# Engine order fixed through v and u of batch 1, and w_out's pieces placed one per two u tiles

## Chip, core, metric

One core of a Trainium2 chip runs the kernel. The metric is the device time of one execution in microseconds; lower is better. The engines are TensorE (PE; its weight loads are PEld), VectorE (DVE), ScalarE (ACT), GpSimd (POOL), and SyncE (SP), which issues the DMAs. Each works through its own list of instructions in order; semaphores make one wait for another.

## What is computed

A retention layer (8 batches, 8 heads, 576 positions, 64 features per head) feeds a gated MLP. Cut to what matters:

```python
scores = q @ k.T / 8                    # per batch and head
ret = (scores * Dmat[h]) @ v            # Dmat: gamma_h ** (i - j) for i >= j, else 0
x = heads side by side                  # (8, 576, 512)
h = np.maximum(x @ w_in, 0.0)           # w_in: 512 x 1024
u, v = h[..., :512], h[..., 512:]
v_n = (v - mean(v)) / np.sqrt(var(v) + 1e-06)        # over the 512 features
v_s = np.einsum('ts,bsd->btd', w_spatial, v_n) + b_spatial[None, :, None]
out = (u * v_s) @ w_out                 # w_out: 512 x 512
```

## The kernel before

Every product of the MLP is done in a reduced float format with each operand split into a high and a low part, and three matmuls (high x high, high x low, low x high; `mm3`) for each pair of tiles. A batch passes these stages:

- *retention* (`scores`, `prep`, `burst`, `evac`): five chunks of up to 128 positions. `burst` is the chunk's group of small matmuls on TensorE; its first ones need the chunk's keys, which GpSimd has scaled in place (`prep`; the tile is `qkv`, the factors `kd`), and `prep` also scales the queries (`qsc`).
- *v* (`v_steps`): blocks of 128 positions (four and a tail of 64, block 4). A block is 12 matmuls of 512 columns (8 for the tail) into one PSUM buffer `v_b_sb`, then seven steps on the same buffer: Relu (ACT), `BN_STATS` and `BN_AGGR` (DVE), root of the variance (ACT) and `mean - v` (ACT), the reciprocal and three small products for the scale (DVE; tile `sm`), the high part of the normalized v (ACT, tile `vn0`), and the low part (DVE, tile `vn1`). With this last step the buffer is free. The tail block adds two halves first and writes `vt1`, `vt2`.
- *u* (`u_tile`): eight tiles of 128 features x 288 positions, 12 matmuls each into a PSUM buffer, then a Relu on ScalarE which empties it.
- *vs* (`vs_mm`) and *f* (`f_stage`): the spatial product with the gate, and the product with `w_out`, eight tiles each.

v, u, vs and f share four PSUM buffers (pool `ps_m`, 512 columns each). A tile's first matmul waits until the tile that had the buffer before is done with it.

The weights come as 64-bit floats and are turned into the high and low format on the chip, in pieces of 128 columns: `front` (absolute value of the high words on ScalarE, a clamp on GpSimd), `mid` (three bit operations on VectorE, tile `f`), `back` (a cast to the high part on ScalarE, the low part on GpSimd). `w_out` has four such pieces, numbered 0 to 3, kind 2. They are `f_20` to `f_23` in the lists below, and `wout0`, `wout1` are the high and low results.

Until the end of batch 0's last gated u tile the order of TensorE, VectorE, ScalarE and GpSimd is the order in which the code is written (`Engine` records it as long as `ordered[0]` is true). From line 643 on a scheduler decides, by its own estimate of times, with all instructions behind the written part (`issue_after`); TensorE's retention matmuls keep their program order. Before the change the scheduled part starts ahead of v of batch 1, so in v and u of batch 1 it places the rest of w_out: `wout_work` (lines 631 to 639) gives one of its parts after each of the eight u tiles in program order, but nothing binds it to that place. After u of batch 1 come `f` of batch 0, with the retention of batch 2 woven in (`interleave`), then vs and f of batch 1, and so on to batch 7, which has no retention beside it.

Of the kernel before, what the change touches and what calls it, by code (L numbers as in the profile page):

```python
# [23 lines left out]
NC = S // C  # L24
# [3 lines left out]
NMB = DM // P  # L28
# [5 lines left out]
def retention_gmlp(ctx, tc, qkv, q_x, qk_t, q_xt, v_t, w_in, w_sp, b_sp, w_out, amask, qscale, kdec, sdec, out):  # L34
# [153 lines left out]
    def front(kind, i, clamp=po):  # L188
        words = staged[kind, i].rearrange("p (n two) -> p n two", two=2)
        hw, lw = words[:, :, 1], words[:, :, 0]  # L190
        f = early[:, i] if kind == 1 else sp.tile([P, 512], F32, name=f"f_{kind}{i}", tag="f", bufs=3)
        a = f if clamp is po else ps_m.tile([P, 512], F32, name=f"w_{kind}{i}", tag="m")
        ac.activation(out=a, in_=hw.bitcast(F32), func=AF.Abs)
        if clamp is po:
            po.tensor_scalar(out=a, in0=a, scalar1=2.0 ** -15, scalar2=None, op0=ALU.max)
        part[kind, i] = hw, lw, a, f

    def mid_steps(kind, i):
        hw, lw, a, f = part[kind, i]
        direct = kind == 1 and a is not f  # L200
        ps = a if kind != 1 or direct else ps_m.tile([P, 512], F32, name=f"w_{kind}{i}", tag="m")
        part[kind, i] = f, ps
        fi = ps.bitcast(I32)
        if direct:
            ve.tensor_scalar(out=a, in0=a, scalar1=2.0 ** -15, scalar2=None, op0=ALU.max)
        ve.tensor_scalar(out=fi, in0=a.bitcast(I32), scalar1=3, scalar2=0x3FFFFFFF, op0=ALU.logical_shift_left, op1=ALU.bitwise_and)
        ve.scalar_tensor_tensor(out=fi, in0=hw, scalar=-2 ** 30, in1=fi, op0=ALU.bitwise_and, op1=ALU.bitwise_or)
        yield
        ve.scalar_tensor_tensor(out=fi, in0=lw, scalar=29, in1=fi, op0=ALU.logical_shift_right, op1=ALU.bitwise_or)
        yield  # L210

    def mid(kind, i):
        for _ in mid_steps(kind, i):
            pass

    def back(kind, i, eng=po):
        hi, lo = (w[:, i, DH:] if kind == 1 else w[:, :, i * P:(i + 1) * P] for w in (win if kind < 2 else wout))
        f, ps = (t if kind == 1 else t.rearrange("p (a n) -> p a n", a=NCB) for t in part[kind, i])
        ac.copy(out=hi, in_=ps)
        if eng is po and kind == 1:  # L220
            ac.copy(out=f, in_=ps)
        eng.tensor_tensor(out=lo, in0=f if eng is po else ps, in1=hi.bitcast(F32), op=ALU.subtract)
# [118 lines left out]
    def mm3(ps, w, r, start, stop):  # L341
        pe.matmul(ps, w[0], r[0], start=start, stop=False)
        pe.matmul(ps, w[0], r[1], start=False, stop=False)
        pe.matmul(ps, w[1], r[0], start=False, stop=stop)

    def v_steps(b, sb):
        n = C if sb < NC else TL
        x = xs[b]
        pf = ps_m.tile([P, 512], F32, name=f"v_{b}_{sb}", tag="m")
        ps = pf[:n]  # L350
        t = slice(sb * C, sb * C + n)
        if sb < NC:
            for cb in range(NCB):
                if cb == 2 and (b, sb) == (0, 3):
                    yield
                mm3(ps, [x[:, i, cb, t] for i in range(2)], [win[i][:, cb, DH:] for i in range(2)], cb == 0, cb == NCB - 1)
        else:
            for cb in range(NCB):
                for i in range(2):
                    pe.matmul(pf, xt[:, cb], win[i][:, cb, DH:], start=(cb == 0 and i == 0), stop=(cb == NCB - 1 and i == 1))  # L360
        yield
        if sb == NC:
            tl = wk.tile([P, DH], F32, name=f"vl_{b}", tag="vl", bufs=1)[:TL]
            ac.copy(out=tl, in_=pf[TL:])
            ve.tensor_tensor(out=ps, in0=ps, in1=tl, op=ALU.add)
        ac.activation(out=ps, in_=ps, func=AF.Relu)
        yield
        s6 = wk.tile([P, 6], F32, name=f"s6_{b}_{sb}", tag="s6", bufs=3)[:n]
        ve.bn_stats(out=s6, in_=ps)
        mv = wk.tile([P, 2], F32, name=f"mv_{b}_{sb}", tag="mv", bufs=3)[:n]  # L370
        ve.bn_aggr(out=mv, in_=s6)
        s = wk.tile([P, 5], F32, name=f"sm_{b}_{sb}", tag="sm", bufs=3)[:n]
        ac.activation(out=s[:, 0:1], in_=mv[:, 1:2], func=AF.Sqrt, bias=eps[:n])
        ac.activation(out=ps, in_=ps, func=AF.Identity, scale=-1.0, bias=mv[:, 0:1])
        yield
        r = s[:, 1:2]
        ve.reciprocal(out=r, in_=s[:, 0:1])
        ve.tensor_scalar(out=s[:, 2:3], in0=mv[:, 1:2], scalar1=EPS, scalar2=r, op0=ALU.add, op1=ALU.mult)
        ve.tensor_scalar(out=s[:, 3:4], in0=s[:, 2:3], scalar1=r, scalar2=0.5, op0=ALU.mult, op1=ALU.mult)
        ve.tensor_scalar(out=s[:, 4:5], in0=s[:, 3:4], scalar1=-1.5, scalar2=r, op0=ALU.add, op1=ALU.mult)  # L380
        nrstd = s[:, 4:5]
        if sb < NC:
            hi, lo = vn[0][:, sb], vn[1][:, sb]
        else:
            hi, lo = vt1[:TL], vt1[TL:]
        ac.activation(out=hi, in_=ps, func=AF.Copy, scale=nrstd)
        if sb == NC:
            ac.activation(out=vt2[:TL], in_=ps, func=AF.Copy, scale=nrstd)
        yield
        ve.scalar_tensor_tensor(out=lo, in0=ps, scalar=nrstd, in1=hi.bitcast(F32), op0=ALU.mult, op1=ALU.subtract)  # L390
        yield

    def v_block(b, sb):
        for _ in v_steps(b, sb):
            pass
# [10 lines left out]
    def u_tile(b, db, t):  # L406
        ps = ps_m.tile([P, 512], F32, name=f"u_{b}_{db}_{t}", tag="m")[:, :HALF]
        u_mm(b, db, t, ps)
        u_relu(b, db, t, ps)

    def u_stage(b):
        for db in range(NDB):
            for t in range(2):
                u_tile(b, db, t)
                yield 1.6

    def v_stage(b):
        for sb in range(NC + 1):
            v_block(b, sb)
            yield 2.75 if sb < NC else 1.9  # L420
# [58 lines left out]
    def go(gen, n=1):  # L479
        for _ in range(n):  # L480
            next(gen)
# [32 lines left out]
    v = [v_steps(0, sb) for sb in range(NC + 1)]  # L514
# [113 lines left out]
    gated_u(1, 3)  # L628
    split_g(1)

    def wout_work():
        for i in range(1, NMB):
            if i > 1:
                front(2, i)
                yield
            mid(2, i)
            yield
            back(2, i)
            yield

    work = wout_work()
    g0 = xs[0]
    ordered[0] = False
    for eng in (pe, ve, ac, po):
        ctx.enter_context(tc.issue_after(eng.last))

    for _ in v_stage(1):
        pass
    for _ in u_stage(1):
        next(work, None)  # L650
    for b in range(1, B):
        interleave(main(b), retention(b + 1) if b + 1 < B else [], 50.0 if b > 1 else 40.0, 12.5)

# [76 lines left out]
```

## Time and profile before

| | us |
|---|---|
| executions timed | 556.49, 556.87, 857.03 (median 556.87) |
| the profiled execution | 556.34 |
| its span, first to last instruction | 554.6 |
| granted TensorE clock, mean over the span | 0.988 |

One execution was profiled. A row of the timeline gives the start and the duration of an instruction, or of a few equal ones that follow each other, in us from the span's start, with the engine, the operation and the tiles (output <- inputs, their numbers left out). All instructions stand at line 71, the helper through which they are issued, so they are told apart by their tiles. Square brackets hold the idle time of the engine ahead of the row and what ended it. A row of the windows gives busy time and number of instructions of PE, PEld, DVE, ACT and POOL in a stretch, then the granted TensorE clock, the share of the DMA engines and GB/s.

### The profile page before, as it was taken

What the parts mean: (1) busy time and instruction counts of PE and PEld (TensorE: products, weight loads), DVE (VectorE), ACT (ScalarE), POOL (GpSimd) and SP (SyncE); (2) the same over time, 40 slices, a digit from 0 to 9 for tenths busy, and PEclk for the clock granted to TensorE, in tenths of its full rate; (3) what the DMA queues carried; (4) which work ended last, traced back from release to release, by engine and by line L of the source; (5) the groups of instructions that cost most, each with busy time, mean ns of one, the idle gap of its engine ahead of it and who ended that gap; (6) DMA issues with size and microseconds to landing.
All of it is one profiled execution on the core that took longest, in us unless ns stands there. A gap on an engine that the chain in (4) does not pass through costs nothing.

```text
span 554.6 us, 15310 instructions
## 1 busy us (share of the span) xinstructions
PE 533.7 (96%) x6735; PEld 496.1 (89%) x6735; DVE 272.1 (49%) x588; ACT 207.8 (37%) x447; POOL 135.1 (24%) x133
## 2 busy tenths in 40 slices
PE   5898999499999999999999999999999999999997
PEld 4677998499998899989999899988999899998997
DVE  7786577812632735237351654427353373506240
ACT  4366335532223632236222552226322362226422
POOL 3857759501302120202102120121201122000000
PEclk8999999799999999999999999999999999999999
DMA  8992663004444322533234222342225341020002
GB/s 315 377 330 77 233 186 115 0 12 154 140 130 153 103 80 64 193 116 116 50 96 176 84 96 50 119 158 83 92 52 182 112 153 50 2 76 11 2 1 86
DMA packets 37045, 64.08 MB, mean 116 GB/s; under 512 B 14833, under 2 KB 27249, under 8 KB 33010
## 3 DMA queue, kind: packets, MB, share of 16 engines
q1 hardware_dynamic: 36978, 63.10, 34.5%
q8 instruction: 53, 0.87, 0.6%
q14 instruction: 14, 0.11, 0.1%
HBM read 53.65 MB, written 9.44 MB: 114 GB/s over the span
## 4 chain that ended last, share of the span: by engine, by line
PE 87%; DVE 4%; DMA 4%; ACT 2%; issue 1%; POOL 1%; SPq 0%; ACTq 0%
PE vs L71 22%; PE f L71 19%; PE u L71 18%; PE v L71 14%; PE r L71 14%; DMA qkv<-in_qkv 4%; DVE f L71 2%; DMA raw<-in_w_out 1%; DVE s L71 1%; ACT v L71 1%; DVE sm L71 0%; DVE w L71 0%; DVE vn L71 0%; ACT wtl L71 0%; POOL qsc L71 0%
## 5 line engine op out<-in xcount | busy, mean ns | idle before, releaser
L71 PE MATMUL vs<-wsp,vn 128*128 128x288 f32 x768 | 114.5, 297 | 1.2 <-ACT pre L71 0.5
L71 PE MATMUL u<-x,win 128*128 128x288 f32 x768 | 107.2, 299 | 8.2 <-DVE vn L71 6.6
L71 PEld LDWEIGHTS u<-x,win 128*128 128x128 f32 x768 | 104.3, 190 | 10.2 <-DVE vn L71 7.0
L71 PEld LDWEIGHTS vs<-wsp,vn 128*128 128x128 f32 x768 | 105.3, 188 | 2.9 <-DVE vn L71 0.7
L71 PE MATMUL v<-win,x 128*128 128x512 f32 x384 | 93.3, 398 | 0.0
L71 PE MATMUL f<-g,wout 128*128 128x288 f32 x672 | 92.1, 295 | 0.0
L71 DVE TENSOR_TENSOR at<-r,am 128x1024 f32<-128x1024 f32 (+1 forms) x40 | 44.5, 1113 | 95.2 <-PE r L71 95.2
L71 PEld LDWEIGHTS f<-g,wout 128*128 128x128 f32 x672 | 89.7, 188 | 0.5
L71 PEld LDWEIGHTS v<-win,x 128*128 128x128 f32 x384 | 71.0, 188 | 16.6
L71 POOL TENSOR_TENSOR qsc<-qsc,qs 128x512 f32<-128x512 f32 (+1 forms) x31 | 36.6, 1183 | 189.1 <-DMA qsc<-in_q_x 139.4
L71 PEld LDWEIGHTS r<-qkv 64*64 64x64 f32 x2176 | 45.8, 135 | 13.8 <-issue 6.3
L71 PE MATMUL r<-qkv 64*64 64x64 f32 (+1 forms) x2176 | 52.3, 235 | 5.4 <-POOL qkv L71 3.5
L71 DVE BATCH_NORM_STATS2 s<-v 128x6 f32<-128x512 f32 (+1 forms) x40 | 27.8, 694 | 57.6 <-ACT v L71 56.4
L71 ACT COPY o<-f 128x288 f32<-128x288 f32 x64 | 25.6, 400 | 73.4 <-PE f L71 73.4
L71 ACT CAST g<-vs 128x288 fp32r<-128x288 f32 x56 | 22.3, 399 | 74.2 <-DVE vs L71 73.0
L71 POOL TENSOR_TENSOR qkv<-qkv,kd 128x512 f32<-128x512 f32 x32 | 33.5, 1048 | 34.9 <-DMA qkv<-in_qkv 30.3
L71 ACT CAST x<-r 128x512 fp32r<-128x512 f32 x32 | 18.8, 586 | 59.6 <-DVE st L71 59.6
L71 DVE TENSOR_TENSOR g<-vs,g 128x288 fp32r<-128x288 f32 x56 | 25.6, 457 | 26.3 <-ACT g L71 26.3
L71 PE MATMUL r<-at,qkv 64*64 64x64 f32 (+1 forms) x1152 | 36.9, 225 | 0.5 <-DVE at L71 0.5
L71 DVE TENSOR_TENSOR vs<-vs,u 128x288 f32<-128x288 f32 x56 | 26.0, 464 | 22.7 <-PE vs L71 22.7
L71 POOL TENSOR_TENSOR st<-st,sd 128x256 f32<-128x256 f32 x24 | 14.9, 620 | 86.9 <-DVE st L71 86.8
L71 ACT ACTIVATE u<-u 128x288 f32<-128x288 f32 x56 | 22.4, 408 | 34.3 <-PE u L71 34.1
(73 smaller groups left out, 520.6 us busy)
## 6 DMA issues: line engine op xcount, KB each, us to landing
qkv<-in_qkv SPq DMA_DIRECT2D x31, 1024.0 KB, 5.3
out<-o SPq DMA_DIRECT2D x64, 144.0 KB, 1.8
qsc<-in_q_x SPq DMA_DIRECT2D x24, 256.0 KB, 3.3
raw_v<-in_w_in SPq DMA_DIRECT2D x4, 512.0 KB, 6.6
qkv<-in_qk_t SPq DMA_DIRECT2D x8, 256.0 KB, 3.7
qkv<-in_v_t SPq DMA_DIRECT2D x16, 128.0 KB, 3.2
raw<-in_w_in SPq DMA_DIRECT2D x4, 512.0 KB, 8.9
raw<-in_w_out SPq DMA_DIRECT2D x4, 512.0 KB, 3.6
```

The costliest lines, as they stand in the source:

```text
L71: ins = op(*args, **kw)
```

## The change

The written order now goes on through v and u of batch 1. `go(gen, n)` takes n steps of a generator; `v_steps` yields after the matmuls, after the Relu, after the statistics with root and shift, after the scale and high part, and after the low part. So block sb runs up to its statistics, then block sb - 1 does its low part, then block sb its scale and high part. The `front` of pieces 2 and 3 of w_out follows the last block's high part. The last block's low part stands behind the first u tile, and then w_out's `mid` and `back` alternate behind the following u tiles. The scheduler decides from f of batch 0 on.

```diff
@@ -628,26 +628,27 @@
     gated_u(1, 3)
     split_g(1)
 
-    def wout_work():
-        for i in range(1, NMB):
-            if i > 1:
-                front(2, i)
-                yield
-            mid(2, i)
-            yield
-            back(2, i)
-            yield
-
-    work = wout_work()
     g0 = xs[0]
+    v = [v_steps(1, sb) for sb in range(NC + 1)]
+    for sb in range(NC + 1):
+        go(v[sb], 3)
+        if sb:
+            go(v[sb - 1])
+        go(v[sb])
+    front(2, 2)
+    front(2, 3)
+    for n, _ in enumerate(u_stage(1)):
+        if n == 0:
+            go(v[NC])
+        elif n == 6:
+            back(2, 3)
+        elif n < 7:
+            i = (n + 1) // 2
+            (mid if n % 2 else back)(2, i)
     ordered[0] = False
     for eng in (pe, ve, ac, po):
         ctx.enter_context(tc.issue_after(eng.last))
 
-    for _ in v_stage(1):
-        pass
-    for _ in u_stage(1):
-        next(work, None)
     for b in range(1, B):
         interleave(main(b), retention(b + 1) if b + 1 < B else [], 50.0 if b > 1 else 40.0, 12.5)
 
```

The tiles in the lists below: `v_1_0` to `v_1_4` are batch 1's v blocks, `sm_1_n` and `mv_1_n` their small tiles, `u_1_d_t` its u tiles, all with a running number behind; `u_633` is u's result, `qkv_2_0` the first chunk of batch 2.

ScalarE through the first blocks of v of batch 1, before:

```order
L71 CAST wout0_1054<-f_21_1087 128x4x128
L71 ACTIVATE v_1_0_1239<-v_1_0_1239 128x512
L71 ACTIVATE sm_1_0_1257<-mv_1_0_1255,eps_91 128x1
L71 ACTIVATE v_1_0_1239<-v_1_0_1239,mv_1_0_1255 128x512
L71 ACTIVATE v_1_1_1266<-v_1_1_1266 128x512
L71 ACTIVATE vn0_343<-v_1_0_1239,sm_1_0_1257 128x512
L71 ACTIVATE sm_1_1_1284<-mv_1_1_1282,eps_91 128x1
L71 ACTIVATE v_1_1_1266<-v_1_1_1266,mv_1_1_1282 128x512
L71 ACTIVATE v_1_2_1293<-v_1_2_1293 128x512
L71 CAST wout0_1054<-f_22_1421 128x4x128
L71 ACTIVATE v_1_3_1320<-v_1_3_1320 128x512
```

and now:

```order
L71 ACTIVATE v_1_0_1239<-v_1_0_1239 128x512
L71 ACTIVATE sm_1_0_1257<-mv_1_0_1255,eps_91 128x1
L71 ACTIVATE v_1_0_1239<-v_1_0_1239,mv_1_0_1255 128x512
L71 ACTIVATE vn0_343<-v_1_0_1239,sm_1_0_1257 128x512
L71 ACTIVATE v_1_1_1265<-v_1_1_1265 128x512
L71 ACTIVATE sm_1_1_1283<-mv_1_1_1281,eps_91 128x1
L71 ACTIVATE v_1_1_1265<-v_1_1_1265,mv_1_1_1281 128x512
L71 ACTIVATE vn0_343<-v_1_1_1265,sm_1_1_1283 128x512
L71 ACTIVATE v_1_2_1292<-v_1_2_1292 128x512
```

The casts of w_out are gone from between v's steps, and each block's Relu stands behind the previous block's high part (`vn0`), where Relus of blocks 1 to 3 stood ahead of it.

VectorE in the middle of v of batch 1, before:

```order
L71 TENSOR_SCALAR f_22_1421<-f_22_1421 128x512
L71 TENSOR_SCALAR sm_1_1_1284<-mv_1_1_1282,sm_1_1_1284 128x1
L71 SCALAR_TENSOR_TENSOR f_22_1421<-raw_22_942,f_22_1421 128x512
L71 TENSOR_SCALAR sm_1_1_1284<-sm_1_1_1284 128x1
L71 BN_STATS s6_1_2_1307<-v_1_2_1293 128x6
L71 SCALAR_TENSOR_TENSOR f_22_1421<-raw_22_942,f_22_1421 128x512
L71 TENSOR_SCALAR f_23_1471<-f_23_1471 128x512
L71 TENSOR_SCALAR sm_1_1_1284<-sm_1_1_1284 128x1
L71 BN_AGGR mv_1_2_1309<-s6_1_2_1307 128x2
L71 SCALAR_TENSOR_TENSOR f_23_1471<-raw_23_1052,f_23_1471 128x512 x2
L71 BN_STATS s6_1_3_1334<-v_1_3_1320 128x6
L71 SCALAR_TENSOR_TENSOR vn1_344<-v_1_1_1266,sm_1_1_1284,vn0_343 128x512
```

and now, from block 1's statistics to block 2's scale (the low parts are the rows `vn1_344`):

```order
L71 BN_STATS s6_1_1_1279<-v_1_1_1265 128x6
L71 BN_AGGR mv_1_1_1281<-s6_1_1_1279 128x2
L71 SCALAR_TENSOR_TENSOR vn1_344<-v_1_0_1239,sm_1_0_1257,vn0_343 128x512
L71 RECIPROCAL sm_1_1_1283<-sm_1_1_1283 128x1
L71 TENSOR_SCALAR sm_1_1_1283<-mv_1_1_1281,sm_1_1_1283 128x1
L71 TENSOR_SCALAR sm_1_1_1283<-sm_1_1_1283 128x1 x2
L71 BN_STATS s6_1_2_1306<-v_1_2_1292 128x6
L71 BN_AGGR mv_1_2_1308<-s6_1_2_1306 128x2
L71 SCALAR_TENSOR_TENSOR vn1_344<-v_1_1_1265,sm_1_1_1283,vn0_343 128x512
L71 RECIPROCAL sm_1_2_1310<-sm_1_2_1310 128x1
L71 TENSOR_SCALAR sm_1_2_1310<-mv_1_2_1308,sm_1_2_1310 128x1
L71 TENSOR_SCALAR sm_1_2_1310<-sm_1_2_1310 128x1 x2
```

w_out's bit operations (`f_22`, `f_23`) stood between v's steps, and block 1's low part behind block 3's statistics; now it is behind block 2's statistics, and the bit operations are behind the last block.

GpSimd behind the splitting of batch 0's gate, before:

```order
L71 TENSOR_TENSOR qkv_2_0_1145<-qkv_2_0_1145,kd_75 128x512
L71 TENSOR_SCALAR f_22_1421<-f_22_1421 128x512
L71 TENSOR_SCALAR f_23_1471<-f_23_1471 128x512
L71 TENSOR_TENSOR qkv_2_1_1217<-qkv_2_1_1217,kd_75 128x512
L71 TENSOR_TENSOR wout1_1055<-f_21_1087,wout0_1054 128x4x128
L71 TENSOR_TENSOR qsc_2_1_1219<-qsc_2_1_1219,qs_74 128x512
L71 TENSOR_TENSOR qsc_2_2_1618<-qsc_2_2_1618,qs_74 128x512
L71 TENSOR_TENSOR wout1_1055<-f_22_1421,wout0_1054 128x4x128
L71 TENSOR_TENSOR wout1_1055<-f_23_1471,wout0_1054 128x4x128
```

and now:

```order
L71 TENSOR_SCALAR f_22_1373<-f_22_1373 128x512
L71 TENSOR_SCALAR f_23_1376<-f_23_1376 128x512
L71 TENSOR_TENSOR wout1_1055<-f_21_1087,wout0_1054 128x4x128
L71 TENSOR_TENSOR wout1_1055<-f_22_1373,wout0_1054 128x4x128
L71 TENSOR_TENSOR wout1_1055<-f_23_1376,wout0_1054 128x4x128
L71 TENSOR_TENSOR qkv_2_0_1145<-qkv_2_0_1145,kd_75 128x512
L71 TENSOR_TENSOR qkv_2_1_1217<-qkv_2_1_1217,kd_75 128x512
L71 TENSOR_TENSOR qsc_2_1_1219<-qsc_2_1_1219,qs_74 128x512
L71 TENSOR_TENSOR qsc_2_2_1618<-qsc_2_2_1618,qs_74 128x512
```

All of w_out's clamps and low parts now stand ahead of the scaling of batch 2's keys (`qkv_2_0`), which stood first. TensorE's list and SyncE's list of DMAs have the same order as before. In batches 2, 3, 5 and 6 a `vn` step and the neighbouring step on the retention's state (`st`) changed places on ScalarE and on VectorE.

## Prediction

> **What bounds the kernel now.** I began with the busy times and the costliest groups, to see which engine ends the span and where it waits.
>
> ```profile
> PE 533.7 (96%) x6735; PEld 496.1 (89%) x6735; DVE 272.1 (49%) x588; ACT 207.8 (37%) x447; POOL 135.1 (24%) x133
> ...
> L71 PE MATMUL u<-x,win 128*128 128x288 f32 x768 | 107.2, 299 | 8.2 <-DVE vn L71 6.6
> ```
>
> TensorE is busy for 96% of the 554.6 us, so only its idle time and its slow time can be won. Of the 8.2 us that it idles ahead of u's matmuls, 6.6 end with a write of `vn` by VectorE. TensorE's timeline from batch 1's v to the first burst of batch 2's retention has that wait:
>
> ```profile
> 85.08 11.36 PE L71 MATMUL v<-win,x 128*128 128x512 f32 x48
> 96.28 2.01 PE L71 MATMUL v<-win,xt 128*128 128x512 f32 x8
> 104.89 3.25 PE L71 MATMUL u<-x,win 128*128 128x288 f32 x12 [6.60 <-DVE vn L71]
> 108.79 11.39 PE L71 MATMUL u<-x,win 128*128 128x288 f32 x84 [0.65 <-ACT u L71]
> ...
> 124.30 1.36 PE L71 MATMUL r<-qkv 64*64 64x64 f32 x64
> ```
>
> The columns are start, duration, instructions, and in brackets the idle time ahead. v's matmuls end at 98.29 (96.28 + 2.01). Nothing runs until 104.89. The first u tile (12 matmuls) then takes 3.25 us, and after 0.65 us more of waiting the other seven run through: 11.39 / 7 = 1.63 us each. The windows over the gap show the clock in the column ahead of the DMA share (0.00 there):
>
> ```profile
> 98.30:101.40 3.10, 0.00 (x0) 0.00 (x0) 3.10 (x5) 2.06 (x5) 3.10 (x3) 1.00 0.00 0
> ...
> 104.80:108.20 3.40, 3.25 (x12) 2.90 (x12) 3.20 (x14) 2.06 (x5) 0.77 (x1) 0.50 0.00 0
> ```
>
> The clock is still 1.00 through the first 3.10 us of idling, and 0.50 through the stretch of 3.4 us in which the first u tile runs. So the place loses 6.60 + 0.65 + (3.25 - 1.63) = 8.87 us. No more than this can be won.
>
> Why TensorE waits: there are four PSUM buffers for v and u, and a v block gives its buffer back with its last step, the VectorE write of `vn`. u's first tile needs block 1's buffer. VectorE's timeline shows that step at 104.10, and what stands ahead of it, the w_out pieces (`f`):
>
> ```profile
> 85.65 1.69 DVE L71 TENSOR_SCALAR f<-f 128x512 int32<-128x512 int32 x1
> 87.38 2.82 DVE L71 SCALAR_TENSOR_TENSOR f<-raw,f 128x512 int32<-128x512 int32 x2
> ...
> 100.37 3.20 DVE L71 SCALAR_TENSOR_TENSOR f<-raw,f 128x512 int32<-128x512 int32 x2
> ...
> 104.10 0.73 DVE L71 SCALAR_TENSOR_TENSOR vn<-v,sm,vn 128x512 fp32r<-128x512 f32 x1
> ```
>
> ScalarE, before and behind the gap (the last two rows serve below):
>
> ```profile
> 90.23 0.62 ACT L71 CAST wout<-f 128x512 fp32r<-128x512 f32 x1 [2.64 <-DVE f L71]
> 90.75 0.58 ACT L71 ACTIVATE v<-v 128x512 f32<-128x512 f32 x1
> ...
> 108.54 0.68 ACT L71 ACTIVATE vn<-v,sm 128x512 fp32r<-128x512 f32 x1
> 109.11 0.28 ACT L71 ACTIVATE sm<-mv,eps 64x1 f32<-64x1 f32 x1
> ```
>
> Block 0's Relu starts at 90.75, behind a cast of w_out that waited for VectorE, though its matmuls (a quarter of 11.36 us) were done at about 88. From 100.37 to 103.57 VectorE was at the last piece of w_out, while v's blocks waited.
>
> **The change, part by part.** The instructions are the same; TensorE's and SyncE's order is the same, so no DMA is issued past another. The new order moves three things.
>
> *v without w_out in it.* In the new order each engine runs a block's steps in a fixed chain: Relu, statistics, root and shift, reciprocal and scale, `vn` high on ScalarE, the next block's Relu behind it, and the previous block's `vn` low on VectorE behind the next block's statistics. Batch 7's v runs with nothing beside it, so I take the steps' distances from there. TensorE, ScalarE, VectorE:
>
> ```profile
> 497.91 11.37 PE L71 MATMUL v<-win,x 128*128 128x512 f32 x48
> ```
> ```profile
> 500.97 0.58 ACT L71 ACTIVATE v<-v 128x512 f32<-128x512 f32 x1 [2.42 <-PE v L71]
> ...
> 503.77 0.58 ACT L71 ACTIVATE v<-v 128x512 f32<-128x512 f32 x1 [0.39 <-PE v L71]
> ...
> 511.16 0.58 ACT L71 COPY vl<-v 64x512 f32<-64x512 f32 x1 [0.67 <-PE v L71]
> ...
> 512.54 0.55 ACT L71 ACTIVATE v<-v 64x512 f32<-64x512 f32 x1
> ...
> 516.99 1.26 ACT L71 ACTIVATE vt<-v,sm 64x512 fp32r<-64x512 f32 x2 [0.62 <-DVE sm L71]
> ```
> ```profile
> 502.32 0.18 DVE L71 BATCH_NORM_AGGREGATE mv<-s 128x2 f32<-128x6 f32 x1
> 502.86 0.16 DVE L71 RECIPROCAL sm<-sm 128x1 f32<-128x1 f32 x1 [0.36 <-ACT sm L71]
> ...
> 503.31 0.46 DVE L71 TENSOR_SCALAR sm<-sm 128x1 f32<-128x1 f32 x2
> ...
> 507.95 0.18 DVE L71 BATCH_NORM_AGGREGATE mv<-s 128x2 f32<-128x6 f32 x1
> 508.05 0.72 DVE L71 SCALAR_TENSOR_TENSOR vn<-v,sm,vn 128x512 fp32r<-128x512 f32 x1
> 508.68 0.15 DVE L71 RECIPROCAL sm<-sm 128x1 f32<-128x1 f32 x1
> ...
> 513.85 0.17 DVE L71 BATCH_NORM_AGGREGATE mv<-s 64x2 f32<-64x6 f32 x1
> ...
> 516.45 0.45 DVE L71 TENSOR_SCALAR sm<-sm 64x1 f32<-64x1 f32 x2
> 518.28 0.74 DVE L71 SCALAR_TENSOR_TENSOR vt<-v,sm,vt 64x512 fp32r<-64x512 f32 x1 [1.38 <-ACT vt L71]
> ```
>
> From TensorE's start to block 0's Relu: 500.97 - 497.91 = 3.06. In the new kernel v's matmuls start at 85.08 as before, since all ahead of them is unchanged, so the Relu R0 = 88.14. From Relu to the second statistics step: 502.32 - 500.97 = 1.35. Block 0 has no earlier block's write to place: reciprocal at R + 1.89 (502.86), end of the scale steps at R + 2.80 (503.31 + 0.46), `vn` high 0.09 later (516.45 + 0.45 to 516.99), the next Relu 0.57 after that starts (108.54 to 109.11): R1 = R0 + 3.46 = 91.60. A later block has the previous `vn` low in between: it starts 0.10 behind the statistics (507.95 to 508.05), takes 0.72, and the reciprocal follows 0.63 after its start (508.68). That makes R + 2.08, scale steps until R + 2.99, high part R + 3.08, next Relu R + 3.65. So R2 = 95.25, R3 = 98.90. The previous block's buffer is free at R + 1.35 + 0.10 + 0.72 = R + 2.17: block 0's at 93.77, before block 4 needs it (96.28); block 1's at 97.42, before v ends; block 2's at 101.07.
>
> Block 4: the copy 0.57 behind block 3's high part (101.98) at 102.55; Relu 1.38 later (511.16 to 512.54), 103.93; second statistics 1.31 later (513.85), 105.24; block 3's low part 105.34 to 106.06; scale steps until 105.97 + 0.91 = 106.88; its high part 106.97; its low part 1.29 later (516.99 to 518.28), 108.26 to 109.00.
>
> *u.* TensorE starts 0.06 after a buffer is free (104.10 + 0.73 to 104.89). Tile 1 runs from 98.29 without a wait. Tile 2 starts at 101.13, tile 3 at 106.12, tile 4 at 109.06; with 1.63 us each the idle times are 1.21, 3.36 and 1.31. From tile 5 on the buffers come from u's own Relus, which are ready: the first one stands behind block 4's two high parts (106.97 + 1.26) and two Abs of w_out, which I take at 0.6 each as a high part: about 109.4, against 110.69. Before, tile 4 was the third of the free seven and started at 108.79 + 2 x 1.63 = 112.05. So the gain at tile 4 is 3.0 us, and the same five tiles follow.
>
> *The clock.* The longest gap, 3.36 us, exceeds the 3.10 after which the clock fell before, so I expect half clock once. Bounds: 0 if it lies inside a gap or doesn't come, 1.6 if a whole tile runs in it as before (3.25 - 1.63). If it lies from 106.1 to 109.5, as long as the stretch above, tile 3 takes 1.6 longer, of which the 1.31 gap behind it hides all but 0.3, and tile 4 loses 0.2: I take 0.5. [...]
>
> *w_out's pieces 1 to 3 beside u.* They still lie beside TensorE's work, but the last one now has GpSimd's step on batch 2's keys (`qkv`) queued behind it, which the burst at 124.30 needs. VectorE and GpSimd rows for the same steps, and the cast on ScalarE:
>
> ```profile
> 57.37 0.83 DVE L71 TENSOR_SCALAR f<-f 128x512 int32<-128x512 int32 x1 [1.46 <-POOL f L71]
> 58.23 1.42 DVE L71 SCALAR_TENSOR_TENSOR f<-raw,f 128x512 int32<-128x512 int32 x2
> ...
> 64.92 0.81 DVE L71 TENSOR_SCALAR f<-f 128x512 int32<-128x512 int32 x1
> 65.76 1.71 DVE L71 SCALAR_TENSOR_TENSOR f<-raw,f 128x512 int32<-128x512 int32 x2
> ```
> ```profile
> 55.85 2.95 POOL L71 TENSOR_SCALAR f<-f 128x512 f32<-128x512 f32 x2 [0.64 <-ACT f L71]
> ...
> 95.36 1.21 POOL L71 TENSOR_TENSOR qkv<-qkv,kd 128x512 f32<-128x512 f32 x1
> ...
> 104.30 1.26 POOL L71 TENSOR_TENSOR wout<-f,wout 128x512 fp32r<-128x512 f32 x1 [1.28 <-ACT wout L71]
> ```
> ```profile
> 103.61 0.62 ACT L71 CAST wout<-f 128x512 fp32r<-128x512 f32 x1 [1.74 <-DVE f L71]
> ```
>
> VectorE starts piece 1 at 108.26 + 0.63 = 108.89, beside two GpSimd clamps (2.95 us): 2.28 as from 57.37 to 59.65. Pieces 2 and 3 beside a GpSimd product: 2.55 each, as from 64.92 to 67.47. Piece 3 ends at 116.27; cast 0.03 + 0.62, GpSimd 0.07 + 1.26, then the keys 1.21: 119.46. The burst is due at 124.30 - 2.5 = 121.8, so 2.3 us are left and this costs nothing. If that cover goes, it becomes the rivals below. The two Abs and three casts on ScalarE only delay u's Relus; the latest that matters, tile 4's behind piece 1's cast, comes near 112.3, and tile 8 needs it at 115.6.
>
> In four of the later batches two neighbours on ScalarE and VectorE (a state copy or sum and a `vn` step) change places. Both orders are there before the change, and TensorE never waited ahead of u elsewhere (8.2 - 6.6 - 0.65 leaves 0.95 us for all other batches together): nothing.
>
> **Sum.** 3.0 - 0.5 = 2.5 us off the profiled execution of 556.34 (554.6 of span and 1.7 around it): 553.8. Of the three runs shown two, 556.49 and 556.87, are 0.15 and 0.53 above that execution (the third, 857.03, stands far off), so I expect a median 0.35 higher: 554.2.
>
> **Rivals.**
> 1. v's chain keeps TensorE's pace. In batch 7 the Relus of blocks 0 and 1 start 2.80 apart (500.97, 503.77), where I count 3.46 and 3.65. At 2.84 (11.36 / 4) block 4's steps come 2.2 earlier and the gain is 5.2: 551.5. Against it: there the next Relu stands ahead of the high part, here behind it.
> 2. VectorE and GpSimd exclude each other over w_out, and the keys come as late as before. Then nine VectorE steps (3 x (0.83 + 1.42) = 6.75), the clamps (2.95) and two products (2.52) run one after another: 108.89 + 12.22 = 121.11, and 3.19 for cast, product and keys gives 124.30, no gain: 556.7. Against it: 58.23's two steps took 1.42 while the clamps ran on until 58.80. [...]
> 3. Slower. Each piece takes what the first one took from 85.65 to 90.20, 4.55, beside unbroken GpSimd products. Then piece 3 ends at 122.54 and the keys at 125.73, 1.4 us after the old burst: 558.1. It decides once piece 3 ends after 121.11. Against it: only two products of 1.26 stand there now.
>
> **How the numbers follow.** The forecast 0.73, rival 1 0.08, rival 2 0.12, rival 3 0.07. The forecast's own range, with the clock's bounds and the runs' scatter, is 553.2 to 555.5. The range 551.5 to 557.0 takes in rivals 1 and 2 and leaves out rival 3. About 2% (11 us) is what a measurement of this kernel can tell from no change; the whole loss here is 8.87, so faster 0.01, same 0.98, slower 0.01.
>
> **What would show it.** In the changed profile: block 0's Relu near 88.1, Relus 3.5 to 3.7 apart, u's tiles 2, 3 and 4 starting near 101.1, 106.1 and 109.1, one short stretch of half clock between 103 and 111, GpSimd's keys done near 119.5, the burst near 121.8. Relus 2.8 apart would make it wrong towards faster; a burst that waits for the keys, towards slower.

## Result and the profile after

The changed kernel took a median of 555.39 us (553.98 to 557.98), the kernel before 558.82 us over as many runs. One execution of the kernel before, at 857.03 us, is left out of the ratio of the means, which is 0.995, 95% interval 0.9934 to 0.9967: about 2.8 us faster. The medians lie 3.4 us apart. The profiled execution took 554.95 us, its span is 553.2 us.

From the page of the profile after, the busy times and the group of u's matmuls:

```profile
PE 535.4 (97%) x6735; PEld 498.1 (90%) x6735; DVE 269.8 (49%) x588; ACT 208.3 (38%) x447; POOL 133.3 (24%) x133
...
L71 PE MATMUL u<-x,win 128*128 128x288 f32 x768 | 108.6, 301 | 5.5 <-DVE vn L71 3.2
```

The idle time ahead of u's matmuls fell from 8.2 to 5.5 us, and what ends with a write of `vn` from 6.6 to 3.2 us. TensorE's timeline after (start, duration, instructions, in brackets the idle time ahead and what ended it):

```profile
85.11 11.36 PE L71 MATMUL v<-win,x 128*128 128x512 f32 x48
...
98.15 1.75 PE L71 MATMUL u<-x,win 128*128 128x288 f32 x12
101.32 1.83 PE L71 MATMUL u<-x,win 128*128 128x288 f32 x12 [1.42 <-DVE sm L71]
106.33 12.47 PE L71 MATMUL u<-x,win 128*128 128x288 f32 x72 [3.19 <-DVE vn L71]
...
122.92 1.36 PE L71 MATMUL r<-qkv 64*64 64x64 f32 x64
```

TensorE no longer stops for 6.60 us and then for 0.65, but for 1.42 and 3.19 us, and from u's third tile on the 72 matmuls of six tiles follow each other. The burst comes 37.81 us after v's start (122.92 - 85.11), where it was 39.22 (124.30 - 85.08): 1.41 us earlier. ScalarE's rows of v, the Relus and the high part between two of them:

```profile
88.16 0.58 ACT L71 ACTIVATE v<-v 128x512 f32<-128x512 f32 x1 [1.69 <-PE v L71]
...
91.06 0.69 ACT L71 ACTIVATE vn<-v,sm 128x512 fp32r<-128x512 f32 x1 [0.49 <-DVE sm L71]
91.65 0.59 ACT L71 ACTIVATE v<-v 128x512 f32<-128x512 f32 x1
...
95.32 0.59 ACT L71 ACTIVATE v<-v 128x512 f32<-128x512 f32 x1
...
98.99 0.59 ACT L71 ACTIVATE v<-v 128x512 f32<-128x512 f32 x1
```

The Relus stand 3.49, 3.67 and 3.67 us apart, each right behind the previous block's high part (the first at 91.06). Before, block 0's Relu came at 90.75; now it comes at 88.16. VectorE at the end of v and in w_out:

```profile
108.45 0.74 DVE L71 SCALAR_TENSOR_TENSOR vt<-v,sm,vt 64x512 fp32r<-64x512 f32 x1 [1.38 <-ACT vt L71]
109.23 0.75 DVE L71 TENSOR_SCALAR f<-f 128x512 int32<-128x512 int32 x1
110.01 1.71 DVE L71 SCALAR_TENSOR_TENSOR f<-raw,f 128x512 int32<-128x512 int32 x2
...
115.13 2.39 DVE L71 SCALAR_TENSOR_TENSOR f<-raw,f 128x512 int32<-128x512 int32 x2
```

GpSimd's steps on batch 2's first keys:

```profile
119.48 2.05 POOL L71 TENSOR_TENSOR qkv<-qkv,kd 128x512 f32<-128x512 f32 x2
```

Block 4's low part, which frees the buffer for u's tile 4, ends at 109.19 (108.45 + 0.74), and w_out's bit operations start behind it. The first of the two key steps (2.05 us together) ends near 120.5, 2.4 us before the burst. The windows show the clock in the column ahead of the DMA share:

```profile
105.00:106.00 1.00, 0.00 (x0) 0.00 (x0) 0.97 (x3) 0.33 (x2) 0.00 (x0) 0.71 0.00 0
112.00:113.00 1.00, 1.00 (x9) 1.00 (x8) 0.96 (x2) 0.79 (x2) 0.59 (x2) 0.88 0.00 0
```

The clock fell at about 105.42 (0.71 over the microsecond from 105 is 0.42 at full and the rest at half clock) and came back at about 112.24: half clock (0.50 in between) for 6.8 us, from the wait ahead of tile 3 on.

### The profile page after: what moved, and what is told of

Its sections match the earlier page's. It is cut to its first block, busy times and chain, and to the rows that moved or that the text cites. A ratio compares the mean times of both kernels' runs of the same rounds, so it can differ in the third digit from the quotient of the medians.

```text
span 553.2 us, 15312 instructions
## 1 busy us (share of the span) xinstructions
PE 535.4 (97%) x6735; PEld 498.1 (90%) x6735; DVE 269.8 (49%) x588; ACT 208.3 (38%) x447; POOL 133.3 (24%) x133
## 4 chain that ended last, share of the span: by engine, by line
PE 87%; DMA 4%; DVE 4%; ACT 2%; POOL 1%; issue 1%; SPq 0%; ACTq 0%
PE vs L71 22%; PE f L71 19%; PE u L71 18%; PE v L71 15%; PE r L71 14%; DMA qkv<-in_qkv 4%; DVE sm L71 1%; DMA raw<-in_w_out 1%; DVE s L71 1%; ACT v L71 1%; ACT vn L71 1%; DVE vn L71 1%; POOL qsc L71 0%; DVE w L71 0%; POOL qkv L71 0%
## 5 line engine op out<-in xcount | busy, mean ns | idle before, releaser
L71 PE MATMUL u<-x,win 128*128 128x288 f32 x768 | 108.6, 301 | 5.5 <-DVE vn L71 3.2
L71 PEld LDWEIGHTS u<-x,win 128*128 128x128 f32 x768 | 105.7, 192 | 7.4 <-DVE vn L71 3.4
L71 PEld LDWEIGHTS r<-at,qkv 64*64 64x64 f32 (+1 forms) x1152 | 31.5, 138 | 2.8 <-DVE at L71 0.6
```

The lines of the kernel that those rows point to most:

```text
L71: ins = op(*args, **kw)
```

## Experiments

Every kernel was timed beside the kernel before, and the ratio is to that. Starts of v differ by up to 1.5 us between executions, so the traces are compared from v's start. The table has all of them:

| kernel | median us | ratio, 95% interval | v's start to the burst | v's start to the span's end |
|---|---|---|---|---|
| before | 558.82 | 1 | 39.22 | 469.52 |
| changed | 555.39 | 0.995, 0.9934 to 0.9967 | 37.81 | 468.09 |
| changed, once more | 555.73 | 0.9938, 0.9919 to 0.9958 | 37.06 | 467.30 |
| idle matmuls in the gaps | 554.74 | 0.9938, 0.9919 to 0.9957 | 36.50 | 466.77 |
| keys first | 555.12 | 0.9939, 0.9918 to 0.9961 | 36.48 | 466.72 |
| order fixed in v alone | 554.68 | 0.9933, 0.9913 to 0.9953 | 36.76 | 467.05 |
| low part at once | 555.94 | 0.9956, 0.9941 to 0.997 | 37.72 | 468.04 |
| order fixed, w_out in v | 561.57 | 1.0053, 1.0033 to 1.0073 | 43.96 | 474.18 |
| next Relu ahead | 550.73 | 0.9867, 0.9845 to 0.9889 | 32.77 | 463.00 |
| Relu ahead, tail spread | 547.78 | 0.98, 0.978 to 0.9819 | 33.38 | 460.30 |
| the same, keys first | 548.47 | 0.9817, 0.9797 to 0.9838 | 30.06 | 460.98 |
| scheduler in v, w_out behind v | 547.96 | 0.9813, 0.9796 to 0.983 | 30.07 | 460.35 |

**Order fixed, w_out in v.** The changed kernel with w_out's pieces back in v, in a written order: piece 1 ahead of block 0, pieces 2 and 3 behind the statistics of blocks 1 and 2.

```diff
+    front(2, 2)
+    front(2, 3)
+    mid(2, 1)
+    back(2, 1)
     for sb in range(NC + 1):
...
             go(v[sb - 1])
+        if sb in (1, 2):
+            mid(2, sb + 1)
+            back(2, sb + 1)
         go(v[sb])
-    front(2, 2)
-    front(2, 3)
...
```

> The changed kernel's fixed order of v's steps, but w_out's pieces 1, 2 and 3 back in v: piece 1 ahead of block 0, pieces 2 and 3 behind the statistics of blocks 1 and 2. Theory: the gain comes from taking w_out's VectorE steps out of v, so this loses it and more, since the Relus are 3.6 us apart plus some 3 us for each piece: block 0's Relu near 90.8, u's second tile near 110, the burst near 130, 5 us slower than before. Rival: fixing the order by itself brings the gain; then the burst stays within 1 us of 122.9.

It is slower than the kernel before, by 3.0 us by the ratio where 5 were expected. ScalarE's rows show why:

```profile
90.40 0.62 ACT L71 CAST wout<-f 128x512 fp32r<-128x512 f32 x1 [2.67 <-DVE f L71]
90.93 0.58 ACT L71 ACTIVATE v<-v 128x512 f32<-128x512 f32 x1
...
94.42 0.59 ACT L71 ACTIVATE v<-v 128x512 f32<-128x512 f32 x1
...
98.41 0.62 ACT L71 CAST wout<-f 128x512 fp32r<-128x512 f32 x1 [1.58 <-DVE f L71]
...
99.88 0.59 ACT L71 ACTIVATE v<-v 128x512 f32<-128x512 f32 x1
```

Block 0's Relu waits again behind a cast of w_out, which waited 2.67 us for VectorE, and the third Relu stands 5.46 us behind the second (99.88 - 94.42), with a cast ahead of the high part. From v's start to the burst it takes 6.15 us longer than with the pieces behind v (43.96 - 37.81). With w_out in these places the written order gains nothing; that w_out left v does.

**Order fixed in v alone.** v written out as in the change, u and w_out left to the scheduler. Since all that it orders is bound behind the written part, w_out's pieces stand behind v here too; batch 2's keys (at 91.12) it puts ahead of them.

```diff
     for sb in range(NC + 1):
         go(v[sb], 3)
         if sb:
             go(v[sb - 1])
         go(v[sb])
...
+    go(v[NC])
     ordered[0] = False
...
+    work = wout_work()
+    for _ in u_stage(1):
+        next(work, None)
```

> The order is fixed through v of batch 1 alone; u and w_out's pieces 1 to 3 are left to the scheduler. Theory: all of the gain comes from v, and the places of w_out's pieces between the u tiles bring nothing: block 3's low part near 105.6 as in the changed kernel, u's fourth tile near 109, burst within 1 us of 122.9 (the clock's stretch may lie otherwise). Rival: the place of one piece per two u tiles matters; then u's tiles or the burst come 2 us or more later.

It took 554.68 us, the changed kernel's time, and its Relus stand 3.5 to 3.7 us apart as there. That a piece goes with every two u tiles is worth nothing; that none goes into v is what counts.

**Idle matmuls in the gaps.** The changed kernel with 4, 11 and 4 matmuls of 512 columns, whose result nobody uses, behind u's first, second and third tile, so that TensorE hardly idles in the gaps ahead of the next tiles.

```diff
+    def fill(k):
+        for _ in range(k):
+            pe.matmul(banks[0][:, 0], win[0][:, 0, :P], xs[1][:, 0, 0, :512], start=True, stop=True)
...
     for n, _ in enumerate(u_stage(1)):
+        fill((4, 11, 4)[n] if n < 3 else 0)
```

> The changed kernel with 4, 11 and 4 idle matmuls (128x512, into a retention bank that is free) behind the first, second and third u tile of batch 1. Theory: the clock fell in the 3.19 us gap and made the six tiles behind it take 12.4 us where 6 x 1.63 and a wait of 1.3 would be 11.1; with the gaps filled the clock stays at 1.00, tile 4 starts near 109.2, the burst of batch 2 near 121.4 instead of 122.92, about 1.5 us faster than the changed kernel. Rival: the tiles wait for something else than the clock; then filling the gaps leaves the burst at 122.9 or later.

TensorE's timeline with the idle matmuls (`r<-x,win`):

```profile
86.33 11.36 PE L71 MATMUL v<-win,x 128*128 128x512 f32 x48
...
104.22 2.69 PE L71 MATMUL r<-x,win 128*128 128x512 f32 x11
107.56 1.85 PE L71 MATMUL u<-x,win 128*128 128x288 f32 x12 [0.65 <-DVE vn L71]
...
110.48 8.23 PE L71 MATMUL u<-x,win 128*128 128x288 f32 x60 [0.16 <-DVE vt L71]
...
122.83 1.36 PE L71 MATMUL r<-qkv 64*64 64x64 f32 x64
```

The clock stayed at 1.00 through v and u. Tile 4 starts 24.15 us after v (110.48 - 86.33) and the burst comes after 36.50. The changed kernel's profiled execution took 37.81, so half clock cost it 1.31 us. The time was 554.74 us, within the scatter of the changed kernel, where 1.5 us less than its time was expected: not every execution pays so much.

**The changed kernel, once more, and keys first.** The changed kernel was run again, and with it a kernel in which GpSimd scales batch 2's first keys ahead of w_out's work instead of behind it.

```diff
+    prepped = set()
     def prep(b, c):
+        if (b, c) in prepped:
+            return
+        prepped.add((b, c))
...
+    prep(2, 0)
     for sb in range(NC + 1):
         go(v[sb], 3)
```

> The changed kernel unaltered, timed on the same chip as the three below. About 0.995 of the kernel before (555.5 to 556.5). From the start of v's matmuls to the burst 36.5 to 37.8 us, by how much half clock falls into the gaps; first keys (qkv) done about 35.4 after v's start.

> The changed kernel, with GpSimd's step on batch 2's first keys (qkv) ahead of w_out's clamps and low parts instead of behind them. If v's buffers pace the place and the keys have some 2 us to spare, as the theory has it: the keys end by 93, the burst stays 36.5 to 37.8 us behind v's start, and the time is that of the changed kernel within 1 us. If the keys, queued behind w_out, hold the burst (the second and third rivals): 1 to 3 us faster than the changed kernel.

The second execution of the changed kernel, TensorE and one window:

```profile
84.90 11.36 PE L71 MATMUL v<-win,x 128*128 128x512 f32 x48
...
106.11 2.56 PE L71 MATMUL u<-x,win 128*128 128x288 f32 x12 [3.17 <-DVE vn L71]
109.03 8.82 PE L71 MATMUL u<-x,win 128*128 128x288 f32 x60 [0.35 <-DVE vt L71]
...
121.96 1.36 PE L71 MATMUL r<-qkv 64*64 64x64 f32 x64
```

```profile
110.00:111.00 1.00, 1.00 (x8) 1.00 (x8) 0.97 (x2) 0.19 (x1) 1.00 (x2) 0.81 0.00 0
```

Here the clock came back at about 110.38 (0.81 over the microsecond from 110 is 0.38 at half clock), 1.35 us after tile 4's start, and the burst came after 37.06 us: half clock cost 0.56. In the first trace it came back 3.0 us after the time at which tile 4 could start (85.11 + 24.13 = 109.24) and cost 1.31. In the kernel with the keys first the cost was nothing (36.48 against 36.50): the clock was back at 109.8, about when tile 4 started. So half clock cost a little under half of the time for which it lasted behind tile 4's start in the two traces that paid for it. What lies ahead of that start cost next to nothing, since a slower tile 3 only fills the wait behind it: with the keys first about 3.4 us at half clock (106.34 to 109.76) lay there. TensorE's instructions up to the burst are the same in all three, and in the kernel with the order fixed in v alone, which paid 0.26 (36.76 - 36.50) with the clock back at about 111.17, 1.2 us behind the end of block 4's low part there: less than that share.

GpSimd with the keys first:

```profile
90.84 1.06 POOL L71 TENSOR_TENSOR qkv<-qkv,kd 128x512 f32<-128x512 f32 x1
```

The first keys are done by 91.90, and nothing else changed: 555.12 against 555.73 us. The keys held nothing up.

**Low part at once.** The changed kernel, with each block's low part right behind its own high part.

```diff
     for sb in range(NC + 1):
-        go(v[sb], 3)
-        if sb:
-            go(v[sb - 1])
-        go(v[sb])
+        go(v[sb], 5 if sb < NC else 4)
```

> The changed kernel, with v's low part right behind its own high part, not behind the next block's statistics. Theory (block 4's last step sets the end; the blocks' distance of 3.5 to 3.7 us is set by the chain from Relu to the next Relu, which this leaves as it is, since VectorE has 1.3 us free there): the buffers of blocks 2 and 3 come free 1 to 2.5 us earlier, tile 2 starts without a wait, tile 3 near 18.5 us after v's start, but tile 4 still near 24 us; burst 36.2 to 38.0 us behind v's start, depending on where half clock falls; time that of the changed kernel within 1.5 us. Rival: the place of the low part paces the blocks, and the time moves by more than 2 us.

```profile
85.06 11.36 PE L71 MATMUL v<-win,x 128*128 128x512 f32 x48
...
98.11 3.68 PE L71 MATMUL u<-x,win 128*128 128x288 f32 x24
103.53 1.85 PE L71 MATMUL u<-x,win 128*128 128x288 f32 x12 [1.74 <-DVE vn L71]
109.03 9.63 PE L71 MATMUL u<-x,win 128*128 128x288 f32 x60 [3.65 <-DVE vt L71]
```

In TensorE's timeline tiles 1 and 2 now run without a wait, tile 3 starts 18.47 us after v (21.22 in the profile after), and tile 4 after 23.97. The waits moved from 1.42 and 3.19 us to 1.74 and 3.65, their end stayed, and so did the time (555.94). The place of the low part, one of the three things that the change names, is worth nothing: the chain from Relu to Relu and the tail block behind it set the end.

**Next Relu ahead.** The changed kernel with one thing exchanged on ScalarE: the next block's Relu stands ahead of the previous block's high part.

```diff
     for sb in range(NC + 1):
-        go(v[sb], 3)
+        go(v[sb], 2)
         if sb:
             go(v[sb - 1])
         go(v[sb])
+        if sb:
+            go(v[sb - 1])
+    go(v[NC])
```

> The changed kernel with one more move: each block's Relu goes ahead of the previous block's scale and high part, as the scheduler has it in batch 7. Theory: what is left of the gap comes from the chain Relu to Relu of 3.67 us against 2.84 us of matmuls a block; with the Relu ahead the Relus come 2.8 us apart (88.2, 91.0, 93.8, 96.6), u's second tile has no wait, the third and fourth wait 0.8 and 1.4 us, the clock stays at 1.00 and the burst starts near 117.5: 5 us faster than the changed kernel and 6.5 to 7 faster than before. Rival: VectorE's own work paces the blocks; then the Relus stay over 3.4 us apart and the burst within 1 us of 122.9.

ScalarE and TensorE:

```profile
88.45 0.58 ACT L71 ACTIVATE v<-v 128x512 f32<-128x512 f32 x1 [1.69 <-PE v L71]
...
91.25 0.58 ACT L71 ACTIVATE v<-v 128x512 f32<-128x512 f32 x1 [0.39 <-PE v L71]
91.75 0.68 ACT L71 ACTIVATE vn<-v,sm 128x512 fp32r<-128x512 f32 x1
...
96.80 0.58 ACT L71 ACTIVATE v<-v 128x512 f32<-128x512 f32 x1 [0.39 <-PE v L71]
```

```profile
98.44 3.34 PE L71 MATMUL u<-x,win 128*128 128x288 f32 x24
102.91 1.85 PE L71 MATMUL u<-x,win 128*128 128x288 f32 x12 [1.13 <-DVE sm L71]
105.82 8.23 PE L71 MATMUL u<-x,win 128*128 128x288 f32 x60 [1.06 <-DVE vt L71]
```

The Relus stand 2.74 to 2.81 us apart, the pace of TensorE's blocks (11.36 / 4 = 2.84), two u tiles run without a wait, and the others wait 1.13 and 1.06 us. By the ratio this is 7.4 us faster than before (6.2 to 8.7), and from v's start to the span's end 5.1 us shorter than the changed kernel (468.09 - 463.00).

**Relu ahead, tail spread.** In addition block 3's two parts stand ahead of block 4's Relu, block 4's steps lie between u's first tiles, so that u's Relus aren't behind them, and w_out comes later. The second kernel has the keys first as well.

```diff
-    for sb in range(NC + 1):
+    for sb in range(NC):
...
+    go(v[NC - 1], 2)
+    us = u_stage(1)
+    go(us)
+    go(v[NC])
+    go(us)
+    go(v[NC])
+    go(us)
+    go(v[NC], 2)
     front(2, 2)
     front(2, 3)
...
```

> Next block's Relu ahead of the high part, and in addition block 3's high and low parts ahead of block 4's Relu, block 4's steps spread between u's first tiles so that u's Relus are early, w_out's pieces 1 to 3 behind. Without any stall TensorE would need about 30.0 us from v's start to the burst (13.04 for v, 12.73 for u, 4.19 for what follows). Theory: u's waits go, but w_out's chain now ends so late that the keys, queued behind it on GpSimd, end about 32.6 after v's start: the burst waits for the keys and the time stays within 1 us of the kernel with the Relu alone ahead (0.987 of before, 550 to 552). Rival: the buffers still pace u, the burst comes without a wait for qkv.

> The same with the keys (qkv) ahead of w_out's work on GpSimd. Theory: the burst comes 30.0 to 30.5 after v's start, 2 to 2.7 us earlier than in the kernel with w_out's work ahead of the keys, 8 to 9 us faster than before: 0.984, about 549 to 550. Rival: if the buffers still pace u, both spread kernels take the same time.

TensorE without the keys first:

```profile
98.74 12.90 PE L71 MATMUL u<-x,win 128*128 128x288 f32 x96
...
112.40 6.75 PE L71 MATMUL f<-x,wout 128*128 128x288 f32 x49
119.08 1.36 PE L71 MATMUL r<-qkv 64*64 64x64 f32 x64
```

u's waits went, as expected, but the first kernel was about 3 us faster (550.73 - 547.78) than with the Relu alone ahead, not equal, and the keys first brought nothing. Both spread kernels take the same time, as the rival had it, but not for its reason, since u has no waits. The expectation took it that the burst stays behind 24 matmuls of f and waits for the keys. It stands behind 49 here: f is ordered by the scheduler, which put more of f ahead of the burst, so TensorE had work until GpSimd was done with the first keys, near 118.8 (the two key steps ran from 117.73 for 2.05 us). The burst's distance from v is no measure of this kernel; the distance to the span's end (460.30) is.

**Scheduler in v, w_out behind v.** The kernel before with one edge added on each of two engines: on VectorE and ScalarE w_out's remaining pieces stand behind v's last step. v itself is left to the scheduler.

```diff
     for _ in v_stage(1):
         pass
+    marking[0] = False
     for _ in u_stage(1):
-        next(work, None)
+        with ExitStack() as late:
+            for eng in (ve, ac):
+                late.enter_context(tc.issue_after(eng.last))
+            next(work, None)
```

Here `eng.last` is also kept for instructions that aren't ordered, until `marking[0]` is false.

> The kernel before, with w_out's pieces 1 to 3 bound behind v's last step on VectorE and ScalarE, and v left to the scheduler, which then puts the Relu of block 1 ahead of block 0's high part. If w_out's leaving v is what gains, and the written order of v's own steps costs, as the theory has it: first Relus 2.8 apart, 32.5 to 33.5 us from v's start to the burst, 0.985 to 0.989 of before (551 to 553), as with the Relu written ahead. If the written order of v is needed for the gain: no better than the changed kernel, 36.5 us or more, 0.994 or above.

ScalarE, TensorE, and the group of u's matmuls on the page:

```profile
88.31 0.58 ACT L73 ACTIVATE v<-v 128x512 f32<-128x512 f32 x1 [1.69 <-PE v L73]
...
91.11 0.58 ACT L73 ACTIVATE v<-v 128x512 f32<-128x512 f32 x1 [0.39 <-PE v L73]
91.61 0.69 ACT L73 ACTIVATE vn<-v,sm 128x512 fp32r<-128x512 f32 x1
```

```profile
85.25 11.36 PE L73 MATMUL v<-win,x 128*128 128x512 f32 x48
...
98.30 12.90 PE L73 MATMUL u<-x,win 128*128 128x288 f32 x96
...
115.32 1.36 PE L73 MATMUL r<-qkv 64*64 64x64 f32 x64
```

```profile
L73 PE MATMUL u<-x,win 128*128 128x288 f32 x768 | 105.5, 296 | 0.9 <-POOL win L73 0.9
```

This went past either expectation. The scheduler puts the next Relu ahead of the high part by itself, and two Relus of u ahead of block 3's high part, and TensorE doesn't wait at all from v to the burst. By the ratio it is 10.4 us faster than before (9.5 to 11.4), about as fast as the spread kernels. The order that the change writes down for v costs most of that: with w_out behind v in both, v written out takes 467.05 us from v's start to the end, the scheduler's v 460.35.

## Why the prediction was right

The time, 555.39 us, lies in the predicted range, 1.2 us above the predicted 554.2, and the gain is 2.8 us by the ratio (1.8 to 3.7) where 2.5 were forecast. Step by step:

- *What bounds the kernel.* Right. The bound of 8.87 us on the place is about what can be won: the kernel with the scheduler in v brings the matmuls behind u 9.15 us closer to v (111.13 - 85.25 = 25.88, before 120.11 - 85.08 = 35.03). The 0.28 more comes from row ends and from 8 tiles in 12.90 us instead of 1.63 each. The timed gain of 10.4 us is above the bound, which was read from one execution of the kernel before with a mean clock of 0.988. Of its 35 executions timed beside the experiments 33 had 0.976 to 0.985, so most had a lower mean clock; in which stages, no trace shows.
- *v without w_out in it.* Right to 0.1 us: Relus at 88.16, 91.65, 95.32 and 98.99, predicted 88.14, 91.60, 95.25 and 98.90. Putting w_out back took 6.15 us away; the chain with the Relu behind the high part was the pace, since exchanging these two freed 5 us.
- *u.* Right in kind, a little large: tile 3 was forecast at 106.12 and came at 106.33, and the gain at tile 4, forecast at 3.0, is 2.82 in the trace without half clock (24.15 us after v, before 112.05 - 85.08 = 26.97).
- *The clock.* That half clock would come once was right. The reason, a gap longer than the 3.10 us after which the clock fell before, was not: it fell 2.27 us into the 3.19 us gap in the first trace (105.42 - 103.15), and in the second at 106.96, 0.85 us after the gap had ended at 106.11. The size in the profiled execution was off too: "I take 0.5" measured 1.31, below the upper bound of 1.6. "one short stretch of half clock between 103 and 111" lasted until 112.24. But the four traces with the same instructions on TensorE gave 1.31, 0.56, 0.26 and 0. That 0.5 stands near their middle is in part luck, since nothing in the one trace could tell where the fall would lie. This is part of why the first trace shows 1.41 us of gain and the timed runs 2.8.
- *w_out's pieces.* Too small, without effect. Piece 3 was forecast to end at 116.27 and ended at 117.52 (115.13 + 2.39), since the two operations beside GpSimd's products took 2.4 us instead of 1.71. The row at 65.76, from which 1.71 was taken, had a GpSimd product beside it only until 66.20, so it lay beside one for a part of its time. The keys were done near 120.5 instead of 119.46, and the slack took it, as keys first showed.
- *The later batches.* Right: ahead of u's matmuls 0.9 us of idle time are left for all of them (5.5 - 1.42 - 3.19), as before.
- *The median.* "0.35 higher" than the profiled execution was too little: over more runs the kernel before stands at 558.82, 2.5 us above its profiled 556.34. That, not the gain, makes up the 1.2 us between forecast and time. And "About 2% (11 us) is what a measurement of this kernel can tell from no change" was too coarse: over these runs the interval of the ratio, 0.9934 to 0.9967, leaves out 1.
- *The rivals.* Rival 1, v at TensorE's pace, was refuted for this change and then made: with the Relu ahead the blocks keep 2.8 us, and more came of it (7.4 us) than the 5.2 it priced: it had block 4's steps come 2.2 us earlier, and tile 4, which waits for the last of them, came 3.7 us earlier (24.15 - 20.42). Rivals 2 and 3 fall with the keys first. That VectorE and GpSimd exclude each other over w_out, as rival 2 had it, no run shows. What the runs show is that the pair of operations takes longer beside GpSimd's work: beside the clamps the pair from 110.01 took 1.71 us, beside products 2.4, and alone, in the kernel with w_out in v, 1.42. The pair from 110.01 to 111.72 and the clamps (109.09 to 112.05) ran at the same time.

## What to carry to other kernels

When a scheduler has put foreign work into a chain of small steps that hold buffers, first try an edge that keeps this work out, before you write the chain's order out: here the edges alone gave 10.4 us, and the written order, which does the same and also puts each Relu behind the previous block's high part, gave 2.8. A written order reached the same time with the next Relu ahead and the tail spread (547.78 against 547.96). In a written order look for the step that the slowest engine waits for next, and put it ahead of steps whose result isn't due yet. A step can come some microseconds earlier without any gain when a later wait ends where it did (with the low part at once tile 3 came 2.75 us earlier, tile 4 did not), so ask of each edit whether the last wait's end moves.

## What the runs showed of the hardware

In v and u of batch 1 half clock lasted multiples of about 3.4 us: 6.8 us in the first trace of the changed kernel (105.42 to 112.24), 3.4 in the second (106.96 to 110.38), 6.8 in the kernel before (101.40 to 108.22) and 17.1 in the kernel with w_out in v (101.42 to 118.48). Its place against the same gaps differed from execution to execution: the fall came 20.31 us behind v's start in the first trace of the changed kernel and 22.06 in the second. The stretch ahead of the fall was not idle throughout: at 105.42 the clock fell though the 3.4 us ahead of it held matmuls from 102.0 to 103.15, about 1.1 us, and it did not come back after the next 3.4 us, which held 2.5 us of them:

```profile
102.00:105.40 3.40, 1.15 (x9) 0.91 (x7) 1.35 (x2) 1.84 (x3) 0.00 (x0) 1.00 0.00 0
105.40:108.80 3.40, 2.47 (x10) 2.47 (x11) 1.88 (x8) 2.47 (x5) 0.00 (x0) 0.50 0.00 0
108.80:112.20 3.40, 3.40 (x16) 3.38 (x15) 3.30 (x5) 2.11 (x6) 2.96 (x2) 0.50 0.00 0
```

Only after the third, busy all through, did it return. In the second execution the stretch from 106.96 to 110.38, at half clock, held 3.06 us of matmuls, and the clock returned behind it. What makes the clock fall and return, these traces do not show.
